# Where ScalarE's copy of a w3 w_out tile stands in its queue: ahead of or behind the exponents of the next weights

## The chip, the cores and the metric

The kernel runs on one core of one Trainium2 chip. The metric is the device time of the whole kernel in microseconds (us), from one launch with all inputs in HBM to the finished output in HBM. All arithmetic on the data is float32, apart from integer operations that take the weights apart.

The core's engines work side by side and are tied by semaphores: TensorE (PE in the profile, PEld for its weight loads) multiplies matrices into PSUM; VectorE (DVE), ScalarE (ACT) and GpSimd (POOL) do the elementwise work; SyncE (SP) issues most of the transfers.

## The reference

```python
# attention block, B, H, S, D = 8, 8, 576, 64
scores = scale * np.matmul(q, k.transpose(0, 1, 3, 2))
ret = scores * Dmat                      # causal decay gamma ** (row - column)
attn_out = np.matmul(ret, v)

# FFN block: 4608 tokens, d_model 512, d_ff 1024
x = attn_out.transpose(0, 2, 1, 3).reshape(B * S, H * D)
a = x @ w1
b = x @ w2
h = a * b @ w3
out = (h @ w_out).astype(np.float32)
```

Two facts carry the part that is changed. First, nothing nonlinear stands between `w3` and `w_out`, so that `(a*b) @ w3 @ w_out` is `(a*b) @ (w3 @ w_out)`. The kernel multiplies the two weights once, into `w3o` (1024 x 512), and uses the product for all tokens. Second, the weights arrive as float64. The kernel loads each weight as a pair of 32-bit integers, and VectorE and ScalarE build the float32 value from its exponent, its mantissa and its sign.

## The kernel before

The program is one long hand-ordered list: each engine executes its instructions in the order in which the Python code emits them. The first quarter converts the weights, starts the attention and the first FFN tiles, and makes `w3o`. The rest alternates attention chunks with the FFN products of the tokens (`up` for a and b, `down` for the product with `w3o`, both in a Strassen-like scheme with seven products).

The weights come in 40 pieces of 128 x 512 values: 16 of w1 and w2, 8 of w_out, and 16 of w3, two for each of the eight 128-row tiles `ft` of w3. The conversion is a Python generator. Each `yield` is one step; other parts of the program pull so many steps at a time, to lay VectorE's conversion work between their own.

```python
    def begin_block():                       # 3 steps
        n = begun[0]
        t = live["raw", n]
        lo, hi = t[:, :, 0], t[:, :, 1]
        e = raw.tile([P, CV], I32, tag="exp", name="e")      # two buffers
        m = raw.tile([P, CV], I32, tag="man", name="m")      # two buffers
        vec = nc.vector
        vec.tensor_scalar(out=e, in0=hi, scalar1=1, scalar2=21,                       # L370
                          op0=ALU.logical_shift_left, op1=ALU.logical_shift_right)
        yield
        vec.tensor_scalar(out=m, in0=hi, scalar1=0x000FFFFF, scalar2=0x00100000,      # L374
                          op0=ALU.bitwise_and, op1=ALU.bitwise_or)
        yield
        vec.scalar_tensor_tensor(m.bitcast(F32), in0=lo.bitcast(U32), scalar=2.0 ** -32, in1=m,   # L377
                                 op0=ALU.mult, op1=ALU.add)
        nc.scalar.activation(e, e, relu, bias=lim[:, 0:1], scale=-1.0)                # L380
        nc.scalar.activation(e, e, relu, bias=lim[:, 1:2], scale=-2.0 ** 23)          # L381
        begun[0] += 1
        yield

    def end_block():                         # 2 steps, 3 for a tile's second piece
        ...
        vec.scalar_tensor_tensor(e, in0=hi, scalar=-(1 << 31), in1=e, ...)            # L391
        yield
        while not (... key[1] < multiplied[0] + 3):
            yield "wait"
        ...
        vec.scalar_tensor_tensor(out, in0=m, scalar=2.0 ** -20, in1=e, ...)           # L402
        if key[0] == "w3" and key[2] == DF // CV - 1:
            yield
            t = pools["wst"].tile([P, KF, P], F32, tag="w3T", name="w3T", bufs=3)
            vec.transpose(...)                                                        # L406
            live["w3T", key[1]] = t
        converted[0] += 1
        if n >= 4:
            load_block()                     # the raw piece five ahead
        ...
        yield

    def conversion():
        yield from begin_block()
        while converted[0] < len(blocks):
            if begun[0] < len(blocks) and converted[0] not in (1, 2, 3):
                yield from begin_block()     # one piece is always begun ahead
            yield from end_block()
            ...
```

So ScalarE turns the integer exponents of a piece into the bits of a float32 power of two, in two operations (L380, L381), after VectorE's L370 of that piece and before its L391. One w3 tile takes 3 + 2 + 3 + 3 = 11 steps.

The product of one tile of w3 with w_out, and the loop that runs through the eight tiles:

```python
    def w3_mm(ft):
        ps = acc.tile([P, DM], F32, tag="acc", name="ps")      # one of seven PSUM buffers
        for g in range(KF):
            nc.tensor.matmul(ps, live["w3T", ft][:, g, :], live["wo"][:, g, :],       # L452
                             start=(g == 0), stop=(g == KF - 1))
        nc.scalar.copy(live["w3o"][:, ft, :], ps)                                     # L454
        multiplied[0] += 1

    ...
    todo = [(0, 1, 2), (0, 0, 3), (0, 1, 3)] + [(0, 2, fp) for fp in range(NQ - 1)]
    while multiplied[0] < KF:
        ft = multiplied[0]
        done = at["w3", ft, DF // CV - 1] + 1
        ready = converted[0] >= done
        if todo:
            first = converted[0] < 4 * NQ
            up(*todo.pop(0), conv=2 if first else 1)
            convert(0 if first else 3)
        if ready or not todo:
            convert_up_to(done)
            w3_mm(ft)
        if not todo:
            convert(11)
    w3_part.close()
    ...
    aside.extend(w3_sums())                  # four sums of blocks of w3o, VectorE, L540
    ahead((2, 0), (2, 1), 1)
    up(0, 2, NQ - 1)
    down((2, 0), (2, 1), ((0, 0), (0, 1)))
    ...
    for g in (NC, NC + 1):
        load(g, "kqv")                       # next attention chunks, into memory that raw, e and m held
```

`up` makes seven products on TensorE (L497), each added on by VectorE (L502) or copied by ScalarE (L510, L517); after each addition it takes one waiting sum from `aside`. `down` multiplies with `w3o` and the four sums (L603).

Of the kernel before, what the change touches and what calls it, by code (L numbers as in the profile page):

```python
# [40 lines left out]
def kernel(  # L41
# [13 lines left out]
    nc = tc.nc  # L55
# [49 lines left out]
    live = {}  # L105
# [324 lines left out]
    def go_on():  # L430
        while converting:
            r = next(converting[-1], "end")
            if r != "end":
                return r
            converting.pop()
        return "end"

    def convert(n):

        for _ in range(n):  # L440
            if go_on() is not None:
                return

    def convert_up_to(n):
        while converted[0] < n:
            assert go_on() is None


    def w3_mm(ft):
        ps = acc.tile([P, DM], F32, tag="acc", name="ps")  # L450
        for g in range(KF):
            nc.tensor.matmul(ps, live["w3T", ft][:, g, :], live["wo"][:, g, :],  # L452
                             start=(g == 0), stop=(g == KF - 1))
        nc.scalar.copy(live["w3o"][:, ft, :], ps)  # L454
        multiplied[0] += 1

    every = [(i, n) for i in range(NB2) for n in range(NB)]

# [273 lines left out]
# [8 lines that stand above are left out]
            convert(0 if first else 3)  # L740
        if ready or not todo:
            convert_up_to(done)
            w3_mm(ft)
        if not todo:
            convert(11)
    w3_part.close()


# [15 lines left out]
    todo = [(down, (0, 0), (0, 1)), (down, (1, 0), (1, 1)), (down, (0, 2), (1, 2))]  # L764
# [119 lines left out]
```

## Time and profile before

| what | before |
|---|---|
| time, median of 3 (lowest to highest) | 869.48 us (868.62 to 869.8) |
| profiled execution, span and mean granted TensorE clock | 867.5 us, 0.998 |
| TensorE, weight loads busy | 845.7 us (97%), 771.2 us (89%) |
| VectorE, ScalarE, GpSimd busy | 468.0 us (54%), 185.9 us (21%), 115.3 us (13%) |
| matmuls of w3 w_out (L452) | 128, first and last start at 159.6 and 218.0 us |
| ScalarE's copies of them (L454) | 8, first and last start at 166.7 and 218.6 us, 585 ns each |
| exponents on ScalarE (L380, L381) | 40 of each, median 722 ns each |

The stage in question is the stretch from about 159 to 219 us of the span. The timeline of one engine lists its instructions by start and duration, and in square brackets the idle time before one and what ended it; the sum of waits lists who waited for whom, in total, how often, and the longest; the chain of waits follows the work that ended last back to what released each step.

One `nc.tensor.matmul` in float32 shows as two matmul records in the profile, so a tile of w3 w_out has 16.

### The profile page before, as it was taken

The numbers are of one execution on the slowest core, as the hardware profiler recorded it, in microseconds if no ns is written. First come the engines' busy times: TensorE is split into PE (matmuls) and PEld (weight loads), VectorE is DVE, ScalarE is ACT, GpSimd is POOL, SyncE is SP. The second block draws the span as 40 slices with busy tenths as digits, with TensorE's granted clock in tenths as the row PEclk, the third lists the DMA queues.
The fourth block names the chain that finished last, engine by engine and source line by source line (L and its number), as shares of the span: only waits on it lengthen the run. The fifth ranks groups of instructions, "written<-read, shape, count | busy, mean of one in ns | idle before, by whom it ended". The sixth has DMA issues, their size and how long they took to land.

```text
span 867.5 us, 15264 instructions
## 1 busy us (share of the span) xinstructions
PE 845.7 (97%) x6309; PEld 771.2 (89%) x6309; DVE 468.0 (54%) x789; ACT 185.9 (21%) x374; POOL 115.3 (13%) x91
## 2 busy tenths in 40 slices
PE   5899999999999999999999999999999999999998
PEld 5889999544888999999999999999999999999996
DVE  4799998986643334543544443534553435334343
ACT  3666333343122221101011101111101100011000
POOL 3010020001202223202023030230400101000000
PEclk9999999999999999999999999999999999999999
DMA  9993453444235534516142335061300000000001
GB/s 192 227 212 115 99 98 98 122 139 74 43 91 125 113 47 81 96 27 110 32 88 39 64 59 95 28 114 24 58 25 26 1 25 1 25 25 1 25 1 48
DMA packets 194628, 63.19 MB, mean 73 GB/s; under 512 B 176632, under 2 KB 184824, under 8 KB 194560
## 3 DMA queue, kind: packets, MB, share of 16 engines
q1 hardware_dynamic: 161920, 54.07, 29.9%
q10 hardware_dynamic: 32640, 8.16, 5.0%
q8 instruction: 49, 0.80, 0.4%
q14 instruction: 19, 0.16, 0.1%
HBM read 52.76 MB, written 9.44 MB: 72 GB/s over the span
## 4 chain that ended last, share of the span: by engine, by line
PE 86%; DVE 7%; DMA 3%; issue 2%; ACT 1%; SPq 1%; POOL 0%; DVEq 0%; ACTq 0%; POOLq 0%
PE up L497 46%; PE po L603 24%; PE ps L452 4%; PE sc L243 4%; PE xps L300 3%; PE xps L293 2%; PE tp L228 2%; PE st L265 1%; DVE c L502 1%; DMA ld_q<-in_q_dram 1%; DVE e L391 1%; DMA ld_k<-in_k_dram 1%; DVE w L402 1%; DVE pm L246 1%; DVE m L377 1%
## 5 line engine op out<-in xcount | busy, mean ns | idle before, releaser
L502 DVE TENSOR_TENSOR c<-up,c 128x384 f32<-128x384 f32 x240 | 133.3, 555 | 187.5 <-PE up L497 182.3
L497 PE MATMUL up<-xT,wA 128*128 128x192 f32 x1152 | 213.0, 328 | 1.1 <-ACT xT L305 1.1
L497 PEld LDWEIGHTS up<-xT,wA 128*128 128x128 f32 x1152 | 191.8, 191 | 3.6 <-ACT xT L305 1.4
L497 PE MATMUL up<-T,wS 128*128 128x192 f32 x768 | 141.4, 327 | 3.3 <-DVE T L471 2.1
L497 PEld LDWEIGHTS up<-T,wS 128*128 128x128 f32 x768 | 127.8, 191 | 3.8 <-issue 2.4
L603 PE MATMUL po<-w3o,ab 128*128 128x256 f32 x456 | 104.4, 381 | 0.8 <-DVE ab L569 0.5
L603 PEld LDWEIGHTS po<-w3o,ab 128*128 128x128 f32 x456 | 85.8, 190 | 13.1 <-DVE ab L569 0.9
L607 DVE TENSOR_TENSOR ot<-po,ot 128x256 f32<-128x256 f32 x90 | 38.2, 424 | 74.6 <-PE po L603 71.8
L517 ACT COPY c<-up 128x384 f32<-128x384 f32 x48 | 22.9, 477 | 225.9 <-PE up L497 221.7
L497 PE MATMUL up<-xT,wS 128*128 128x192 f32 x384 | 70.7, 327 | 0.6 <-DVE c L502 0.5
L246 DVE TENSOR_TENSOR pm<-sc,mask 128x512 f32<-128x512 f32 (+1 forms) x80 | 45.4, 628 | 46.6 <-PE sc L243 46.6
L497 PE MATMUL up<-T,wA 128*128 128x192 f32 x384 | 70.3, 326 | 0.0
L603 PE MATMUL po<-wB,forms 128*128 128x256 f32 x288 | 65.1, 379 | 0.0
L497 PEld LDWEIGHTS up<-xT,wS 128*128 128x128 f32 x384 | 63.5, 190 | 1.7 <-DVE c L502 1.7
L497 PEld LDWEIGHTS up<-T,wA 128*128 128x128 f32 x384 | 63.7, 190 | 0.0
L214 POOL TENSOR_TENSOR ld_v<-ld_v,gk 128x1024 f32<-128x1024 f32 (+1 forms) x17 | 33.1, 1949 | 213.0 <-DMA ld_v<-in_v_dram 187.9
L603 PEld LDWEIGHTS po<-wB,forms 128*128 128x128 f32 x288 | 54.7, 190 | 7.4
L452 PE MATMUL ps<-wo,w3T 128*128 128x512 f32 x128 | 56.1, 596 | 2.9 <-DVE w3T L406 2.9
L452 PEld LDWEIGHTS ps<-wo,w3T 128*128 128x128 f32 x128 | 23.8, 190 | 34.4 <-issue 30.6
L471 POOL TENSOR_TENSOR T<-xT,T 128x384 f32<-128x384 f32 x20 | 20.9, 1043 | 214.3 <-PE up L497 212.5
L523 DVE TENSOR_TENSOR ab<-c 128x768 f32<-128x768 f32 x48 | 46.5, 968 | 3.8
L510 ACT COPY c<-up 128x384 f32<-128x384 f32 x48 | 22.8, 476 | 117.3 <-PE up L497 68.4
(73 smaller groups left out, 805.8 us busy)
## 6 DMA issues: line engine op xcount, KB each, us to landing
raw<-in_moe_w_dram SPq DMA_DIRECT2D x64, 128.0 KB, 3.0
out_dram<-ot SPq DMA_DIRECT2D x24, 256.0 KB, 2.1
bl_q<-in_q_dram SPq DMA_DIRECT2D x136, 32.0 KB, 2.1
bl_k<-in_k_dram SPq DMA_DIRECT2D x136, 32.0 KB, 2.2
raw<-in_moe_w_dram SPq DMA_DIRECT2D x8, 512.0 KB, 7.3
raw<-in_moe_w_dram SPq DMA_DIRECT2D x16, 256.0 KB, 5.7
ld_k<-in_k_dram SPq DMA_DIRECT2D x8, 512.0 KB, 6.9
ld_q<-in_q_dram SPq DMA_DIRECT2D x8, 512.0 KB, 8.5
```

The lines of the kernel that those rows point to most:

```text
L214: nc.gpsimd.tensor_tensor(out=t, in0=t, in1=gam[:sz, c].unsqueeze(1).unsqueeze(3).to_broadcast([sz, 2, H, D]), op=ALU.mult)
L243: nc.tensor.matmul(sc[j][:sz, p, :sz], kT[hs, b, p, :sz], qT[hs, b, p, :sz], start=True, stop=True)
L246: nc.vector.tensor_mul(pm[:sz, b, j, :, :sz], sc[j][:sz, :, :sz], mask[:sz, :sz].unsqueeze(1).to_broadcast([sz, NP, sz]))
L300: nc.tensor.matmul(banks[r][heads[half], b, n, :sz], vs[:sz, b * H + 2 * p + j, :], pm[:sz, b, j, p, :sz], start=(c == 0 and m == 0), stop ...
L452: nc.tensor.matmul(ps, live["w3T", ft][:, g, :], live["wo"][:, g, :], start=(g == 0), stop=(g == KF - 1))
L497: nc.tensor.matmul(ps[:, w, :], a[:, w, r, :], b[:, r, :], start=(new and w == r == 0), stop=(w == r == 1), skip_group_check=True)
L502: nc.vector.tensor_add(c[:, to], ps, c[:, sb])
L510: nc.scalar.copy(c[:, 0], p1)
L517: nc.scalar.copy(c[:, 0], p1)
L523: nc.vector.tensor_mul(ab[:, 4 * fp:4 * fp + 4, :], c[:, :, 0, :], c[:, :, 1, :])
L603: nc.tensor.matmul(ps[nm], a[A][:, f, :], live["W"][B][:, f, :], start=(f == 0 and not on), stop=(f == NP - 1), skip_group_check=True)
L607: nc.vector.tensor_add(ot[:, to[0], to[1]], ps[nm], ot[:, sb[0], sb[1]])
```

## The change

`w3_mm` no longer emits the copy, but returns it as a function. The loop calls it after the eleven conversion steps that it takes between two tiles. In ScalarE's queue the copy of tile `ft` so comes behind the exponents of the two pieces that these eleven steps begin, and no longer ahead of them. No instruction is added or taken away, and the order on all other engines stays. It is meant to keep the exponents, which VectorE needs for the next tiles, from standing behind a copy that can't start until TensorE has ended its tile.

```diff
@@ -451,8 +451,8 @@
         for g in range(KF):
             nc.tensor.matmul(ps, live["w3T", ft][:, g, :], live["wo"][:, g, :],
                              start=(g == 0), stop=(g == KF - 1))
-        nc.scalar.copy(live["w3o"][:, ft, :], ps)
         multiplied[0] += 1
+        return lambda: nc.scalar.copy(live["w3o"][:, ft, :], ps)
 
     every = [(i, n) for i in range(NB2) for n in range(NB)]
 
@@ -740,9 +740,11 @@
             convert(0 if first else 3)
         if ready or not todo:
             convert_up_to(done)
-            w3_mm(ft)
-        if not todo:
-            convert(11)
+            evict = w3_mm(ft)
+
+            if not todo:
+                convert(11)
+            evict()
     w3_part.close()
```

## The prediction

> **What bounds the kernel now.** I read the busy shares first.
>
> ```profile
> PE 845.7 (97%) x6309; PEld 771.2 (89%) x6309; DVE 468.0 (54%) x789; ACT 185.9 (21%) x374; POOL 115.3 (13%) x91
> ```
>
> TensorE is busy for 97% of the span, so only its idle time can be won by reordering: 867.5 - 845.7 = 21.8 us in all, most of it in the first 60 us. The change touches only the stage of w3 w_out. So I asked next for the waits between 155 and 226 us.
>
> ```profile
> ACT w3o L454 <- PE ps L452: 36.5, 8, 6.3
> ...
> PE ps L452 <- DVE w3T L406: 2.9, 3, 1.3
> DVE e L391 <- ACT e L381: 2.9, 3, 1.1
> ```
>
> ScalarE sits for 36.5 us in front of its eight copies, each time until TensorE has ended the tile. That alone would cost nothing, but VectorE waits three times for exponents (2.9 us), and TensorE three times for a transposed tile (2.9 us). The chain of waits in the same stretch shows how the three hang together:
>
> ```profile
> 167.94 7.12 PE ps L452 x16
> ...
> 175.08 0.59 ACT w3o L454
> 175.66 0.63 ACT e L380
> ...
> 176.32 0.73 ACT e L381
> ...
> 177.07 0.70 DVE e L391
> ...
> 181.45 1.25 DVE w3T L406
> ...
> 182.75 7.15 PE ps L452 x16
> ```
>
> The chain leaves TensorE at the end of tile 1 (I count from 0), passes the copy, two exponent operations and six to eight VectorE operations, and comes back to TensorE at tile 3. The timeline of VectorE shows that the exponents of tile 3 were wanted much earlier:
>
> ```profile
> 170.53 0.43 DVE L370 TENSOR_SCALAR e<-raw 128x512 int32<-128x512 int32 x1
> ...
> 174.55 0.38 DVE L370 TENSOR_SCALAR e<-raw 128x512 int32<-128x512 int32 x1
> ...
> 177.07 0.69 DVE L391 SCALAR_TENSOR_TENSOR e<-raw,e 128x512 int32<-128x512 int32 x1 [1.07 <-ACT e L381]
> ```
>
> Their input, the L370 at 170.53, is there at 170.96. ScalarE begins them at 175.56, because the copy ahead of them waits for the end of tile 1. The copies in ScalarE's timeline then give the pace of TensorE, as each starts when its tile is done:
>
> ```profile
> 166.66 0.58 ACT L454 COPY w3o<-ps 128x512 f32<-128x512 f32 x1 [5.09 <-PE ps L452]
> ...
> 175.08 0.59 ACT L454 COPY w3o<-ps 128x512 f32<-128x512 f32 x1 [5.09 <-PE ps L452]
> ...
> 181.94 0.58 ACT L454 COPY w3o<-ps 128x512 f32<-128x512 f32 x1 [3.54 <-PE ps L452]
> ...
> 189.92 0.58 ACT L454 COPY w3o<-ps 128x512 f32<-128x512 f32 x1 [4.64 <-PE ps L452]
> ...
> 196.88 0.58 ACT L454 COPY w3o<-ps 128x512 f32<-128x512 f32 x1 [3.64 <-PE ps L452]
> ...
> 204.75 0.59 ACT L454 COPY w3o<-ps 128x512 f32<-128x512 f32 x1 [4.54 <-PE ps L452]
> ...
> 211.72 0.58 ACT L454 COPY w3o<-ps 128x512 f32<-128x512 f32 x1 [3.64 <-PE ps L452]
> 218.59 0.58 ACT L454 COPY w3o<-ps 128x512 f32<-128x512 f32 x1 [6.28 <-PE ps L452]
> ```
>
> The distances are 8.42, 6.86, 7.98, 6.96, 7.87, 6.97 and 6.87 us. The last tile had its input long before, so 6.87 us is TensorE's own pace. The excess over it is 1.55, 0, 1.11, 0.09, 1.00, 0.10 and 0, together 3.85 us. Every second tile is late, as a copy alternately finds its tile just done or still running.
>
> [...] the exponents whose input is ready at 170.96 start only behind the copy of 175.08. [...] the sum (L540) at 223.34 took 2.46 us where the others took 1.21 to 1.22, and it ran out the GpSimd scaling of 221.97 to 224.71 (2.74 us where its neighbour took 1.90). [...]
>
> **The change part by part.**
>
> 1. It removes nothing and adds nothing. What it moves is a 0.585 us copy, eight times, behind up to four exponent operations of 0.722 us. From the order of the instructions on ScalarE in the trace: before, copy 0 stands ahead of tile 2's two exponent pairs, copy 1 ahead of tile 3's, up to copy 5 ahead of tile 7's; copies 6 and 7 have none behind them. After, copy 0 stands ahead of tile 3's pairs, copy 1 ahead of tile 4's, up to copy 4 ahead of tile 7's.
>
> 2. **Slack of the exponents.** Tile 3's first pair now has copy 0 ahead of it. Tile 0 is done at 166.66; the copy then waits for tile 2's second pair, whose input (the L370 at 167.72) is there at 168.10 and which ends at about 169.6. Copy 0 runs to about 170.2, and tile 3's pair can start at its own input, 170.96, and end by 172.4. VectorE wants it at 175.31 + 0.61 = 175.92. That is 3.5 us of slack. For later tiles the copy is likewise one tile older, so its TensorE work has ended before the pairs ahead of it have. The three VectorE waits of 1.07, 0.94 and 0.86 us (2.87) should vanish.
>
> 3. **Does TensorE get all of it?** Tile 1's excess of 1.55 us stays: its transposition starts at 166.55, and VectorE was never idle from 155.92 to then, since it also had the last additions of an `up`. Tile 2 had no excess. So what can be won is the rest, 1.11 + 0.09 + 1.00 + 0.10 = 2.30 us.
>
> 4. **VectorE's own pace.** Where VectorE doesn't wait for ScalarE, its transpositions start 6.90 us apart (181.45 to 188.35) and 6.97 us apart (196.28 to 203.25). That is a little above TensorE's 6.87. From tile 2's transposition at 173.38, four steps of about 6.93 lead to 201.10 for tile 6, which ends at 202.35. TensorE would end tile 5 at 175.08 + 4 x 6.87 = 202.56. The margin is 0.21 us. In the trace, margins of 0.32 and 0.25 us (transposition ended at 189.60 and 204.50 against copies at 189.92 and 204.75) went with 0.09 and 0.10 us of excess. I take 0.2 us in total for this. Tile 7 needs fewer VectorE operations, as no piece is begun ahead, and isn't late.
>
> 5. **The later copies cost nothing.** Copies 0 to 5 now start up to 2.5 us after their tile. Their PSUM buffer is one of seven and isn't wanted again until several tiles later; `w3o` is read only after copy 7. That copy has no exponents ahead of it that could still be running: tile 7's last pair needs the L370 at about 202.2.
>
> 6. **Passing it on.** The stage ends at 218.59 - 2.30 + 0.2 = 216.5 instead of 218.59. After 230 us the waits show only some half microsecond of TensorE waiting at any one time (0.5 for L569 at 230.12, later 0.2 and 0.3). The next attention chunks are loaded when the raw pieces are let go, that is by VectorE's L391 of the last tile, so their issue at 207.46 moves ahead with VectorE by 2.87. Their scaling ends at 224.71 and TensorE reads them at 240.7, so transfers don't swallow the gain.
>
> Sum: 2.30 - 0.2 = 2.1 us of 869.48, 0.24%. I predict 867.3 us.
>
> **The rivals.**
>
> A: **VectorE becomes the bound** and takes most of it back. For it: its pace of 6.90 to 6.97 us against 6.87, so the two engines are nearly balanced and every hitch in VectorE shows. Against: TensorE starts tile 2 with 0.4 us of margin, and four tiles at 0.03 to 0.10 us each use up only that. If VectorE's pace were 7.1 us, five tiles would lose 1 us, and the time would be 868.3.
>
> B: **The clash of the sums with GpSimd changes.** VectorE is busy without a break from 221.26 to 230.98, and TensorE waits 0.5 us for its L569. GpSimd's scaling will come up to 2.9 us earlier and the sums 2.1 us earlier, so which pair of instructions meets is open. If none meets, 1.2 us on VectorE and some 0.5 us on TensorE are won on top: 866.8. If two meet, TensorE loses another 1 us: 868.3.
>
> C: **The wait was hidden anyway**, a copy's delay now holds a buffer or the raw loads become the limit, and the time stays at 869.5. Against: the chain of waits runs through the copy three times, and VectorE never waited for a raw piece in this stage.
>
> D: **A worse place**: the exponents of tile 2's second piece come so late that copy 0 and what follows is delayed. Point 2 shows slack of over 3 us, so this would need a different order of instructions from the one I read out of the trace.
>
> **Range and chances.** The mechanism bounds the gain at 2.3 us plus the 0.5 of B, and A or B can halve it. The three times before spread over 1.2 us, so a median moves by some 0.5 us on its own. This gives 866.3 to 868.5. A change of 2% would be 17 us, eight times what the stage holds: within 2% is at 0.985, faster by more 0.01, slower by more 0.005.
>
> **What would show it right or wrong.** Right: VectorE's three waits for L381 are gone; TensorE's waits for w3T shrink from three to the one of 1.31 us at tile 1; the last copy starts near 216.5; ScalarE's wait for L452 falls well below 36.5 us, as only copies 6 and 7 wait long. Step 4 is wrong if the copies' successors stand more than 6.95 us apart on TensorE (by the start of its matmuls), with VectorE busy throughout. Step 6 is wrong if the stage ends 2 us earlier and the kernel doesn't: then a wait of TensorE after 216 us will have grown. The prediction as a whole is wrong if VectorE still waits for exponents.

## The result and the profile after

| | before | after |
|---|---|---|
| time, median of 6 (lowest to highest) | 869.64 us (868.48 to 870.07) | 865.72 us (865.15 to 867.54) |
| ratio to before, 95% interval | | 0.9962 (0.9949 to 0.9975) |
| span of the profiled execution | 867.5 us | 863.2 us |
| first matmul of tile 0 | 159.60 us | 157.62 us |
| start of the copy of tile 7 | 218.59 us | 214.38 us |
| between the two: length of the stage | 58.99 us | 56.76 us |
| from there to the end of the span | 648.9 us | 648.8 us |

The time fell by 3.9 us and not by 2.1: it lies under the stated range, which began at 866.3. The table already divides the 4.3 us by which the two profiled spans differ: 2.23 us lie inside the stage, 0.1 us behind it, and 1.98 us ahead of it, where not one instruction was moved (2.23 + 0.1 + 1.98 = 4.3). The experiments had to settle whether those 2 us belong to the change.

First the page of after, busy shares, and the sum of waits between 155 and 226 us (the copy has moved to L455):

```profile
PE 844.1 (98%) x6309; PEld 770.1 (89%) x6309; DVE 465.6 (54%) x789; ACT 186.5 (22%) x374; POOL 113.7 (13%) x91
```

```profile
ACT e L380 <- DVE e L370: 23.8, 13, 2.6
...
ACT w3o L455 <- PE ps L452: 11.2, 2, 6.3
...
PE ps L452 <- DVE w3T L406: 1.3, 1, 1.3
```

ScalarE now idles for its own input (L370) instead of for TensorE; only two copies, those of tiles 6 and 7, still wait for TensorE. VectorE's line of waits for L381 is gone, and TensorE has one wait for a transposed tile left, the one at tile 1. The chain of waits shows the same from TensorE's side:

```profile
164.56 1.26 DVE w3T L406
...
165.96 48.38 PE ps L452 x112
214.34 2.62 PE up L497 x16
```

Where the chain of before left TensorE every second tile, seven tiles (112 matmul records) now run in one piece. ScalarE's timeline shows the new order at work:

```profile
167.54 0.57 ACT L455 COPY w3o<-ps 128x512 f32<-128x512 f32 x1
169.00 0.72 ACT L380 ACTIVATE e<-e,lim 128x512 int32<-128x512 int32 x1 [0.90 <-DVE e L370]
...
207.51 0.58 ACT L455 COPY w3o<-ps 128x512 f32<-128x512 f32 x1 [4.94 <-PE ps L452]
214.38 0.58 ACT L455 COPY w3o<-ps 128x512 f32<-128x512 f32 x1 [6.28 <-PE ps L452]
```

Copy 0 carries no idle time in brackets: it comes right behind an exponent pair, some 2.9 us after its tile was done (estimated: tile 0 took 166.66 - 159.60 = 7.06 us in the kernel before, so it was done near 157.62 + 7.06 = 164.68). Tile 3's exponents, behind it, start as soon as their L370 has delivered.

### The profile page after: what moved, and what is told of

Read it like the earlier page. It is cut to its first block, busy times and chain, and to the rows that moved or that the text cites. A ratio compares the mean times of both kernels' runs of the same rounds, so it can differ in the third digit from the quotient of the medians.

```text
span 863.2 us, 15264 instructions
## 1 busy us (share of the span) xinstructions
PE 844.1 (98%) x6309; PEld 770.1 (89%) x6309; DVE 465.6 (54%) x789; ACT 186.5 (22%) x374; POOL 113.7 (13%) x91
## 4 chain that ended last, share of the span: by engine, by line
PE 87%; DVE 4%; issue 2%; DMA 1%; SPq 1%; ACT 0%; DVEq 0%; ACTq 0%
PE up L497 45%; PE po L603 25%; PE ps L452 6%; PE sc L243 4%; PE xps L300 3%; PE xps L293 2%; PE tp L228 1%; PE st L265 1%; DVE c L502 1%; SPq L725 0%; DVE e L391 0%; DMA raw<-in_moe_w_out_dram 0%; DVE w L402 0%; DMA gqs<-decay_q_dram 0%; DMA out_dram<-ot 0%
## 5 line engine op out<-in xcount | busy, mean ns | idle before, releaser
L502 DVE TENSOR_TENSOR c<-up,c 128x384 f32<-128x384 f32 x240 | 133.2, 555 | 186.5 <-PE up L497 181.6
L510 ACT COPY c<-up 128x384 f32<-128x384 f32 x48 | 22.9, 476 | 117.5 <-PE up L497 68.0
```

Of the source, the lines that this page charges most:

```text
L502: nc.vector.tensor_add(c[:, to], ps, c[:, sb])
L510: nc.scalar.copy(c[:, 0], p1)
```

## The experiments

Each kernel below was timed beside the kernel before on the same chip. Since the total moves with the start of the program, the length of the stage in each kernel's trace (first matmul of tile 0 to the start of tile 7's copy) is given as well.

| kernel | median us | ratio to before (95% interval) | stage us |
|---|---|---|---|
| after_again | 867.32 | 0.9974 (0.9963 to 0.9984) | 56.72 |
| before_shifted | 868.89 | 0.9995 (0.9987 to 1.0003) | 59.00 |
| between_pairs | 866.68 | 0.9970 (0.9961 to 0.9980) | 56.80 |
| odd_only | 869.06 | 0.9997 (0.9989 to 1.0006) | 58.95 |
| copy_on_dve | 868.88 | 1.0001 (0.9992 to 1.0011) | 59.50 |
| v_on_scalar | 866.53 | 0.9973 (0.9964 to 0.9983) | 56.78 |
| one_step_more | 869.70 | 1.0005 (0.9999 to 1.0011) | 55.13 |
| filled_gap | 865.80 | 0.9965 (0.9952 to 0.9978) | 56.77 |
| filled_slot | 865.98 | 0.9963 (0.9951 to 0.9975) | 56.23 |
| together | 863.84 | 0.9944 (0.9932 to 0.9956) | 56.26 |
| before_filled | 868.11 | 0.9997 (0.9989 to 1.0005) | 59.00 |
| after_filled | 866.20 | 0.9977 (0.9966 to 0.9988) | 56.78 |

### Is the difference all the change's? after_again, before_shifted

The changed kernel once more, and the kernel before with two blank lines.

> The changed kernel once more. The traces of before and after differ by 2.2 us inside the stage of w3 w_out and by 2.0 us ahead of it, in the first 60 us, where no instruction was changed. Theory (the early part is the luck of a run: TensorE's granted clock dips in some starts and not in others, whatever the kernel): the runs fall into two groups some 2 us apart, with mean clocks of about 0.998 and 0.999 or 1.000, in both kernels, and the medians differ by 2.2 us plus or minus what the mix of the groups makes; within a group the difference is 2 to 2.5 us. Rival (the change itself makes the start faster): the whole difference of 3.3 to 4 us comes back with every group.

> The kernel before with two blank lines added, so the same instructions. Theory of luck: the ratio to the kernel before is 1.000 within 0.15%, with both groups of runs present. Rival (each build of a program has a start of its own): the median differs by 1 to 2 us though no instruction differs.

The stage lengths came back to within 0.04 us, the totals did not: the second measurement of the changed kernel is 867.32 us, 2.0 us under the kernel before on its chip. What differs is visible in the stretches of 2.5 us at the start. The columns are the stretch, its length, the busy time of TensorE, its weight loads, VectorE, ScalarE and GpSimd, then the granted TensorE clock, the DMA share and GB/s. Before:

```profile
32.50:35.00 2.50, 1.49 (x7) 1.52 (x8) 2.40 (x6) 2.50 (x10) 0.00 (x0) 0.83 0.99 245
35.00:37.50 2.50, 2.50 (x9) 2.50 (x8) 1.74 (x4) 1.04 (x3) 0.00 (x0) 0.50 1.02 279
37.50:40.00 2.50, 2.50 (x17) 2.50 (x17) 1.93 (x5) 1.15 (x3) 0.00 (x0) 0.98 1.12 204
```

After, the same stretch:

```profile
35.00:37.50 2.50, 2.50 (x15) 2.23 (x15) 2.50 (x6) 1.49 (x5) 0.00 (x0) 1.00 1.07 299
```

In the trace of before TensorE's clock is halved between about 34 and 38 us, and 9 matmuls fit where 15 fit in the other; I call this the dip. By the clock the loss is (0.17 + 0.50 + 0.02) x 2.5 = 1.7 us. The trace of after_again, with the same instructions as after, has the dip as well (0.53 and 0.78 in the last two stretches). So the dip goes with the run, not with the kernel.

The dip is not the whole of the 1.98 us between the two traces. The same group of matmuls starts at 44.81 us in the trace of before and at 43.97 in that of after, a lag of 0.84 us. The rest comes at 58 us, where TensorE waits for a sum of weights (`wS`) that VectorE finishes late. In the trace of before:

```profile
46.61 2.27 DVE L402 SCALAR_TENSOR_TENSOR wA<-m,e 128x512 f32<-128x512 f32 x1
...
58.46 1.54 PE L497 MATMUL up<-T,wS 128*128 128x192 f32 x8 [1.17 <-DVE wS L160]
```

This L402 began 0.76 us into a scaling on GpSimd (45.85 to 48.34 us); the same one took 0.69 us in the trace of after, where both began at 45.77 us and TensorE has no such wait. The wait is 1.30 us in the trace of filled_slot, which has the dip, and 0.34 us in that of after_filled, which has none. Whether the dip brings this wait about was not tested.

A run's mean clock tells the runs with the dip apart: over the 87 runs of the kernel before that were taken beside the first ten kernels of the table, 60 have a mean clock of 0.998 or less and a median of 869.53 us, and 27 have 0.999 or more and 868.16 us. Both groups are there in the shifted kernel too (8 runs at 869.40, 5 at 867.91). For the changed kernel, first and second measurement together, they are 9 runs at 867.48 and 6 at 865.39. Group by group the change is worth 2.05 us with the dip and 2.77 without; the second figure rests on only six runs of the changed kernel. In the first measurement four of six runs of after had no dip, while the median of before, 869.64 us, is close to that of runs with it. That mix is where the larger part of the surplus came from.

### Which part of the order matters? between_pairs, odd_only

```diff
-            if not todo:
-                convert(11)
-            evict()
+            if not todo:            # between_pairs
+                convert(4)
+            evict()
+            if not todo:
+                convert(7)
```

> The changed kernel with the copy between the two exponent pairs instead of behind both. Tile 3's first pair then comes ahead of copy 1, its second behind it. Theory (VectorE's slack decides): copy 1 starts when tile 1 is done, the second pair ends about 2.0 us later, and VectorE wants it about 3.6 us later, so nothing is lost: the stage ends 2.2 us earlier than before, as with the whole change. Rival (each pair behind the copy costs its share): half of it, 1.1 us.

The whole gain is there (56.80 us). In ScalarE's timeline the pair behind the copy follows it at once, and the next copy waits 2.63 us for TensorE. VectorE has no wait for L381 in this trace:

```profile
176.07 0.59 ACT L455 COPY w3o<-ps 128x512 f32<-128x512 f32 x1 [2.61 <-PE ps L452]
176.55 0.72 ACT L380 ACTIVATE e<-e,lim 128x512 int32<-128x512 int32 x1
...
182.94 0.58 ACT L455 COPY w3o<-ps 128x512 f32<-128x512 f32 x1 [2.63 <-PE ps L452]
```

What decides is not how many exponents stand behind a waiting copy, but whether they are done before VectorE wants them.

```diff
-            if not todo:
-                convert(11)
-            evict()
+            if ft % 2 == 0:         # odd_only
+                evict()
+            if not todo:
+                convert(11)
+            if ft % 2:
+                evict()
```

> The changed kernel with only the copies of odd tiles deferred. In the kernel before only copies 1, 3 and 5 made VectorE wait. Theory (the copies of even tiles were early only because the odd ones had delayed the stage): once tile 3 is on time, copy 2 waits for tile 2 and tile 4's exponents wait behind it, so VectorE waits twice by 0.9 to 1.2 us, now for tiles 4 and 6, and only 0.2 to 0.5 us of the 2.2 are left. Rival (each late copy had a cost of its own): the whole 2.2 us remain, as the three copies that cost are deferred.

All of the gain is gone, even more than expected: 58.95 us against 58.99. VectorE's waits in this kernel:

```profile
184.09 0.69 DVE L391 SCALAR_TENSOR_TENSOR e<-raw,e 128x512 int32<-128x512 int32 x1 [1.04 <-ACT e L381]
198.99 0.69 DVE L391 SCALAR_TENSOR_TENSOR e<-raw,e 128x512 int32<-128x512 int32 x1 [1.00 <-ACT e L381]
```

The exponents wait behind the copies of tiles 2 and 4, which start when TensorE is done:

```profile
182.09 0.58 ACT L455 COPY w3o<-ps 128x512 f32<-128x512 f32 x1 [5.03 <-PE ps L452]
182.57 0.72 ACT L380 ACTIVATE e<-e,lim 128x512 int32<-128x512 int32 x1
```

These two copies had cost nothing in the kernel before. A wait that was cured at one tile came up at the next, and a reading that charges each late copy with a cost of its own is refuted.

### How near is VectorE to being the bound? copy_on_dve

```diff
-        return lambda: nc.scalar.copy(live["w3o"][:, ft, :], ps)
+        return lambda: nc.vector.tensor_copy(live["w3o"][:, ft, :], ps)
```

> The changed kernel with the eight copies on VectorE, at the same places of the order. It asks how near VectorE is to being the bound of the stage. Theory (VectorE needs 6.90 us a tile against TensorE's 6.87, with 0.4 us of margin at tile 2): a PSUM copy of about 0.6 us a tile makes 7.5 us, so the start of tiles 3 to 6 falls behind by about 0.6 us each; the stage gets 2.4 to 3.2 us longer than in the changed kernel and ends about where the kernel before ended it. Rival (there is room on VectorE): the stage stays as long as in the changed kernel, within 0.5 us.

The stage became 2.74 us longer than in the changed kernel, and the total is about that of before. VectorE's timeline:

```profile
171.40 0.68 DVE L455 COPY w3o<-ps 128x512 f32<-128x512 f32 x1
174.50 1.25 DVE L406 STREAM_TRANSPOSE w3T<-w 128x1024 f32<-128x1024 f32 x1
...
181.94 1.25 DVE L406 STREAM_TRANSPOSE w3T<-w 128x1024 f32<-128x1024 f32 x1
```

The transpositions are 7.44 us apart, no copy waits until tile 6, and TensorE waits 0.2 to 0.4 us for the transposition ahead of each of tiles 2 to 6. VectorE is the bound there; there is no room on it for half a microsecond a tile.

### Does the clash behind the stage cost anything? v_on_scalar

```diff
-            scale(g + 1, "v")
+            scale(g + 1, "v", g == NC)     # True: eight multiplications on ScalarE
```

> The changed kernel with one scaling of v taken from GpSimd to ScalarE (eight operations there), the one that ran beside the four sums of w3o and stretched one of them from 1.21 to 2.36 us. Theory (the sums are VectorE's critical chain until TensorE's first product with w3o): all four sums take 1.21 us, TensorE's waits for L569 go (0.5 us, 0.9 us by its weight loads), and the stretch from the last tile's end to there gets 0.5 to 0.9 us shorter. Rival (TensorE waits for something else just behind it): the sums get faster and nothing comes of it.

In the changed kernel one of the four sums was stretched, as in the kernel before, only another one: the first, which began while GpSimd's scaling was running:

```profile
216.90 1.90 POOL L214 TENSOR_TENSOR ld_v<-ld_v,gk 128x1024 f32<-128x1024 f32 x1 [0.21 <-DMA ld_v<-in_v_dram]
...
217.52 2.36 DVE L540 TENSOR_TENSOR w3o<-w3o 128x1024 f32<-128x1024 f32 x1
...
225.81 3.72 PE L603 MATMUL po<-w3o,ab 128*128 128x256 f32 x16 [0.50 <-DVE ab L569]
```

With the scaling on ScalarE all four sums take 1.22 us, and TensorE goes through its first products with `w3o` without a break:

```profile
219.72 1.22 DVE L540 TENSOR_TENSOR w3o<-w3o 128x1024 f32<-128x1024 f32 x1
...
225.48 5.34 PE L603 MATMUL po<-w3o,ab 128*128 128x256 f32 x24
```

From tile 7's copy to the second of these products it was 225.81 - 214.38 = 11.43 us. It is now 225.48 - 216.58 + 1.73 = 10.63 us (1.73 us for the first eight of the 24 records: a third of the 5.18 us after which the next group starts, at 230.66). All nine runs had a mean clock of 0.998 or less; their median of 866.53 stands against 867.48 of the changed kernel's runs of that kind. The 0.8 us are passed on to the total.

### Can tile 1's wait be had as well? one_step_more, filled_slot

```diff
-            convert(0 if first else 3)
+            convert(0 if first else 4)      # one_step_more
```

> The changed kernel with four conversion steps instead of three after each product set of the stretch ahead of the stage, to fill VectorE's idle 1.0 and 0.84 us there. Theory (tile 1's wait of 1.3 us comes from VectorE arriving late): tile 1 is transposed 1 to 2 steps earlier, the wait shrinks to 0 to 0.6 us, and 0.7 to 1.3 us are gained over the changed kernel. Rival (VectorE's idle time there is fixed by waits): the additions to c are delayed by the added steps, TensorE waits for them, and nothing or less than nothing is gained.

The stage lost all its waits (55.13 us), and the kernel still was no faster than before. TensorE's timeline, two of its lines:

```profile
143.93 1.57 PE L497 MATMUL up<-xT,wS 128*128 128x192 f32 x8 [0.71 <-DVE c L502]
...
164.95 55.10 PE L452 MATMUL ps<-wo,w3T 128*128 128x512 f32 x128
```

The wait for L502 comes back in four product sets: 0.7 us three times, 1.9 once. In the same four sets VectorE now idles 0.84 or 0.85 us until ScalarE's copy L510 is done, as long as in the trace of after only in the last set, and the additions that TensorE needs come late. The rival was right here. The next edit adds one step at a single place, in the last set but one:

```diff
         product(p5, "S4", "B22")
+        if m == 2 and fp == 1:              # filled_slot
+            convert(1)
         plus(p5, 1, 1)
```

> The changed kernel with one conversion step more, at one place only: ahead of the last addition of the last product set but one, where VectorE idles for 1.0 us (at 148.5 in the trace of after). No step is added between the sets, which is where the earlier try did harm. Theory (ScalarE's copy to c stands behind an exponent pair there, as the copies of w3 w_out did the other way round; with the step taken earlier the pair is done sooner): VectorE's idle 1.0 and most of its 0.84 us go, tile 1 is transposed 1.2 to 1.8 us earlier, TensorE's wait at tile 1 of 1.31 us falls to 0 to 0.2, and the stage with the set ahead of it gets 1.1 to 1.5 us shorter than in the changed kernel. Rival (as in the earlier try, TensorE waits for an addition instead): a wait for L502 of 0.5 us or more turns up and the gain is under 0.5 us.

TensorE's wait at tile 1 fell from 1.31 to 0.80 us only:

```profile
168.79 48.36 PE L452 MATMUL ps<-wo,w3T 128*128 128x512 f32 x112 [0.80 <-DVE w3T L406]
```

VectorE's idle 1.00 and 0.84 us became 0.40 and 0.25, but 0.53 us turned up in front of the last addition, which can't come before its product. So 0.5 us were gained in the trace of the 1.1 to 1.5 expected, and no new wait of TensorE's arose. Neither the theory nor its rival foresaw this.

### Where does the dip come from? filled_gap, before_filled, after_filled

```diff
         p1 = product(None, "A11", "B11")
+        if m == fp == 0:                    # results not used
+            fill = acc.tile([P, 2, TB], F32, tag="acc", name="fill")
+            for _ in range(6):
+                nc.tensor.matmul(fill[:, 0, :], A(fp, "A11")[:, 0, 0, :],
+                                 live["B", i, n]["B11"][:, 0, :], start=True, stop=True, ...)
```

> The changed kernel with six matmuls more whose result nobody reads, in TensorE's gap of about 2 us after the first product set's first product (near 31.5 us of the span). It asks where the two groups of runs come from. Theory (some runs take that gap as a lull[...]): with the gap filled no run shows the dip near 35 us, all mean clocks are 0.999 or more, all times lie in the faster group, and the median falls by 1 to 1.7 us against the changed kernel's. Rival (the dip has another cause): both groups of runs are there as before, and the median stays or rises a little.

> The kernel before with the six filling matmuls at the start, so that its runs no longer differ by the dip of the clock. Theory: its median is that of the runs of the kernel before without the dip, near 868.2 us, 1.0 to 1.4 us under the kernel before's overall median.

> The changed kernel with the same six matmuls, beside the one with the order of before. Theory (the change is worth what the stage shows and nothing else): the two medians are 2.0 to 2.5 us apart. Rival (the first comparison's 3.9 us are the change's own): 3 to 4 us apart.

```profile
31.35 2.11 PE L513 MATMUL fill<-xT,wA 128*128 128x192 f32 x12
33.60 1.54 PE L497 MATMUL up<-T,wS 128*128 128x192 f32 x8
```

In TensorE's timeline the added matmuls of filled_gap take the place of the idle 2.09 us. None of the 31 runs with the filling (these three kernels and `together`) had a mean clock under 0.999, against 70 of 106 of the kernel before. The dip needs the gap; that is shown. The gap alone isn't enough: the trace of after has it, 2.09 us long, and no dip. The amount was not as expected for before_filled: its median is 0.4 us under that of before, not 1.0 to 1.4, partly as only 10 of the 19 runs of before beside it had the dip. Without the dip the runs still spread from 867.14 to 869.02 us. What spreads them was not isolated; in three of the four traces with the filling TensorE waits 0.6 to 1.3 us for a transfer of k near 44 us, which it does not in the first two.

The pair answers the main question without the dip: 868.11 and 866.20 us, 1.9 us apart, at stage lengths of 59.00 and 56.78. That is just under the expected 2.0 to 2.5 and far from 3 to 4. It is no sharp figure: after_filled has seven runs, five between 865.81 and 866.34 us and two near 867.54.

### The three additions at once: together

> The changed kernel with three additions at once: the filled slot, the filled gap at the start, and v's scaling on ScalarE. If the three are independent: against the changed kernel's faster group 1.3 us for the slot plus 0.8 us for the sums less clash, so a median near 863.6 us and no run with the dip of the clock. Rival (the gains overlap): the wait of TensorE after the stage returns, and the median stays above 864.5 us.

The slot, the filling and v on ScalarE in the changed kernel: 863.84 us (863.57 to 864.30), the fastest kernel here, 0.9944 (0.9932 to 0.9956) of before. Its trace has both gains of the slot and the sums in full: the stage is 0.5 us shorter, and from tile 7's copy to the second product with `w3o` it takes 10.63 us, as in v_on_scalar. The median is 1.55 us under the 865.39 of the changed kernel's runs without the dip, a little more than 0.5 + 0.8. It comes near the expected 863.6, but with some luck, as 1.3 us had been put down to the slot.

## Why the prediction was right, and where it was not

**Steps 1 and 2**, the order on ScalarE and the slack, held. The three waits of 2.87 us are gone. Tile 3's first pair ended at 169.76 + 0.72 = 170.48, and VectorE's L391 took it up at 173.96: 3.5 us of slack, as worked out, so rival D did not come. between_pairs shows that even half of the move would have done, and odd_only that every copy of the alternating row had to move.

**Step 3**, 2.30 us to be won and tile 1's 1.31 us to stay: the stage is 2.23 us shorter in the first traces and 2.2 to 2.3 us in each later pair, and the 1.31 us are there unchanged.

**Step 4** had the right mechanism and too large a size. VectorE's timeline of after:

```profile
171.40 1.25 DVE L406 STREAM_TRANSPOSE w3T<-w 128x1024 f32<-128x1024 f32 x1
...
178.31 1.25 DVE L406 STREAM_TRANSPOSE w3T<-w 128x1024 f32<-128x1024 f32 x1
...
199.04 1.25 DVE L406 STREAM_TRANSPOSE w3T<-w 128x1024 f32<-128x1024 f32 x1
```

The distance is 6.91 us, not 6.93. Tile 6 was ready at 200.29, and TensorE ended tile 5 at 214.38 - 2 x 6.87 = 200.64: a margin of 0.35 us, where 0.21 was estimated. From tile 1's first matmul to the last copy it is 214.38 - 165.96 = 48.42 us; tile 1 took 175.08 - 167.94 = 7.14 in the kernel before, so the term of 0.2 us measures 48.42 - (7.14 + 6 x 6.87) = 0.06 us. The 6.97 us that I had averaged in came from a stretch where ScalarE still held VectorE up: there an L391 began at 198.88, just behind its exponents' end at 198.13 + 0.72 = 198.85.

**Steps 5 and 6** held. Copies up to 2.9 us late (2.5 in the prediction) cost nothing, and behind the stage the spans differ by 0.1 us. Rival C falls with it.

**Rival A** did not come, but is near: VectorE's 6.91 us a tile stands 0.04 us above TensorE's 6.87, and with 0.53 us more a tile, in copy_on_dve, VectorE set the pace. **Rival B** came out even: two instructions met again, a different pair at the same price (2.36 for 2.46 us).

**The range** is what failed. It let a median move "by some 0.5 us on its own". The start of the program has a dip of TensorE's clock, in some runs and not in others, and the medians of the two groups are 1.4 us apart in the kernel before and 2.1 in the changed one; a median of few runs moves by up to that much. The profile before had shown it: a mean clock of 0.998 is 0.2% of 867.5 us, or 1.7 us, and I did not ask where it was lost. With the changed kernel measured again the time is 867.32 us, beside the 867.3 predicted; that they agree so closely is luck in the mix, as seven of the nine runs had the dip. Like with like is the fairer measure: 2.05 us among runs with the dip, 1.9 with the gap filled in both kernels, where 2.1 were predicted.

## What to carry to other kernels

In a queue that runs in order, as ScalarE's did here (in the kernel before, exponents ready at 170.96 us began at 175.56, behind the copy of 175.08), ask of each instruction that waits long what stands behind it and who needs that; a copy out of PSUM with free buffers can go behind short operations that feed the next tile, as here, up to 2.9 us late at no cost. Move all of an alternating row, not only the ones that show a wait: in odd_only the wait went to the next tiles (1.04 and 1.00 us). Before a gain of a few tenths of a per cent is put down to a change, compare the traces ahead of the first changed instruction.

## What the runs showed of the hardware

TensorE idled for 2.09 us near 33 us in the traces of before, after and filled_slot, after a shorter lull of 0.74 to 1.11 us with one group of matmuls (1.57 us) between the two. In 70 of 106 runs of the kernel before the mean clock points to a dip. Nine traces show one, with 1.70 to 1.73 us lost by the clock in each. In the trace of before the granted clock, in stretches of 0.5 us, was 0.67 from 34 us, 0.50 from 34.5 to 37.5 and 0.92 from 37.5: 1.7 us lost, or some 3.4 us at half speed (estimated from these clocks).

Two things were not shown: why runs of one program differ, as the trace of after has the lull (0.74 us) and the gap (2.09 us) and no dip; and by what the gap, without which none of 31 runs had a dip, leads to one.
